# Attention times V as four column tiles with the attention weights moving, its denominators carried through DRAM, on one Trainium2 core

## The chip, the cores and the metric

The kernel runs on one core of one Trainium2 chip. The metric is the device time of one execution in microseconds (us), as the median of several runs. In these profiles PE is the tensor engine (PEld its weight loads), DVE the vector engine, ACT the scalar engine, POOL the general engine, and SP the engine that issues most DMAs. "L488" is line 488 of the kernel.

## The reference, cut to what matters

```python
x = A_x                                              # [1, 2048, 512], bf16
g = sigmoid((x * gate_w).sum(-1, keepdims=True))     # one gate per token
return g * attention(x) + (1 - g) * ffn(x)

# attention: 32 heads of 16, four segments of 512 tokens, for each segment
logits = einsum('bhqd,bhkd->bhqk', qs, ks) * scale + causal_mask
a_dot  = softmax(logits) @ vs                        # inside the segment
a_mem  = (phi(qs) @ M) / (phi(qs) . z + 1e-6)        # recall of earlier segments
o      = sigmoid(beta) * a_mem + (1 - sigmoid(beta)) * a_dot
M, z   = M + phi(ks)^T @ vs, z + phi(ks).sum()
# then o @ wo; ffn: (relu(x @ W_gate) * (x @ W_up)) @ W_down with 1792 hidden features
```

## The kernel before

A small planner in the kernel holds a list of tasks with engine, assumed duration, assumed latency, priority and dependencies. It fixes the order in which each engine's instructions are emitted. At run time every engine works through its list in that order, so an instruction whose input is late holds back those that follow on its engine (a stall of 6.19 us of this kind is shown below). Attention runs about two "units" (8 heads of one segment; in the trace one starts every 14.8 us on average) ahead of the feed-forward work, which fills the tensor engine.

`exp(logits)` is kept transposed, as E[key, query]. Attention times V takes E as the *stationary* operand and 17 columns (V and a column of ones, which yields the softmax denominator, "den") as the moving one. The result has queries on partitions, so that dens are per-partition columns and the combine is plain vector work:

```python
def pv(p=p, sl=sl):                      # p: half of the four query blocks
    for q2 in range(2):
        qb = 2 * p + q2
        if seg:                          # recall of earlier segments, beside it
            nc.tensor.matmul(wb[sl.banks[1]][:, q2 * 136:(q2 + 1) * 136],
                             lhsT=pqT[u % RQ][:, qb * P:(qb + 1) * P], rhs=mbd[i][:, c], ...)
        for h8 in range(8):
            j, r = divmod(h8, 2)
            for kb in range(qb + 1):
                ...
                nc.tensor.matmul(bank(sl)[:, lo:lo + HW],               # HW = 17
                                 lhsT=E[(5 * u + f) % RE][:, j, o:o + P],
                                 rhs=Vp[i][:, kb, 8 * c + h8, 0:HW], ...)
# comb(): reciprocal of den columns, times gates, times both products, add  (DVE)
# then a DMA transpose of the [query, feature] block into oT, for the matmul with wo
```

The softmax here doesn't subtract the row's maximum and nothing guards it: scores larger than these inputs give would overflow.

## Time and profile before

| | before |
|---|---|
| time, median (range) | 290.53 us (290.47 to 290.75) |
| span of the profiled run | 289.2 us |
| PE busy | 277.7 us, 96% |
| attention times V, first start to next start, summed (L488) | 34.4 us |
| all 512-column matmuls, likewise (L306) | 207 us |
| QK, row-tiled, likewise (L440) | 29.8 us |

Here are lines of the page of the kernel before: busy time per engine, then the busy tenths of PE in 40 slices of the span, the granted clock in tenths, and the chain that ended last by engine.

```profile
PE 277.7 (96%) x2860; PEld 138.3 (48%) x2906; DVE 176.5 (61%) x442; ACT 194.5 (67%) x168; POOL 87.3 (30%) x139
...
PE   8899999999999999999999999999999999899994
...
PEclk9999999999999999999999999999999999999999
...
PE 88%; ACT 3%; DMA 3%; issue 2%; another core or an unknown queue 1%; DVE 1%; SPq 0%; POOL 0%; ACTq 0%
```

PE is busy throughout, at full clock, and it makes up 88% of the chain: time taken from PE should come off the kernel.

The timeline of PE before (start us, duration us, engine, line, operation, out<-in, count) shows what one attention-times-V matmul and one change of tiling mode cost.

```profile
120.38 0.23 PE L479 MATMUL wb_135<-mbd_187,pqT_154 128*128 128x136 bf16 x1
120.45 0.17 PE L488 MATMUL wb_134<-Vp_163,E_82 128*128 128x17 bf16 x1
120.48 0.17 PE L488 MATMUL wb_134<-Vp_163,E_76 128*128 128x17 bf16 x1
120.50 0.17 PE L488 MATMUL wb_134<-Vp_163,E_78 128*128 128x17 bf16 x1
...
121.92 1.02 PE L306 MATMUL wb_133<-wv_sb,xT 128*128 128x512 bf16 x3
122.88 0.40 PE L440 MATMUL sp<-QT_137,KTe_143 32*128 32x384 bf16 x8
123.21 0.39 PE L306 MATMUL wb_132<-xT,wg_sb 128*128 128x512 bf16 x1
```

(Of the group of four that starts at 121.92, one record is missing.) A 17-column matmul takes 0.17 us, but one starts every 25 ns; busy times overlap, so distances between starts are what count. The QK group moves 512 columns in all and takes 0.33 us until the next start, where 512 columns in the plain mode take 0.216.

### The profile page before, as it was taken

How to read it: one execution, taken by the hardware profiler on the slowest of the kernel's cores; microseconds unless marked ns; L12 is line 12 of the kernel's file. 1: busy time of each engine (PE TensorE's matmuls, PEld its weight loads, DVE VectorE, ACT ScalarE, POOL GpSimd, SP SyncE). 2: the span in 40 equal slices, each digit the busy share in tenths (PEclk: the TensorE clock that was granted, in tenths of full speed). 3: DMA queues.
4: the chain of work that ended last, by engine and by line, in shares of the span. 5: the costliest groups of instructions: out<-in, count | busy, mean ns of one | idle time of the engine just before them, and what ended most of it. 6: DMA issues, size and time to landing. Idle time of an engine off the chain costs nothing.

```text
span 289.2 us, 6881 instructions
## 1 busy us (share of the span) xinstructions
PE 277.7 (96%) x2860; PEld 138.3 (48%) x2906; DVE 176.5 (61%) x442; ACT 194.5 (67%) x168; POOL 87.3 (30%) x139
## 2 busy tenths in 40 slices
PE   8899999999999999999999999999999999899994
PEld 4344546454545453545453545346635445544442
DVE  2689895666946168569692658657948434554211
ACT  2389888789865678779866678787796667433100
POOL 5025242333433334333334252423334243200000
PEclk9999999999999999999999999999999999999999
DMA  7999941010200201000103010000100111010011
GB/s 238 315 258 351 205 96 33 3 25 13 40 18 22 57 18 21 20 18 2 36 15 63 20 37 3 18 2 2 20 18 3 36 39 31 7 20 0 0 36 36
DMA packets 33198, 15.91 MB, mean 55 GB/s; under 512 B 22672, under 2 KB 33168, under 8 KB 33168
## 3 DMA queue, kind: packets, MB, share of 16 engines
q1 hardware_dynamic: 31424, 14.42, 20.2%
q10 hardware_dynamic: 1744, 1.06, 1.2%
q8 instruction: 22, 0.36, 0.6%
q14 instruction: 8, 0.07, 0.1%
HBM read 8.14 MB, written 2.10 MB: 35 GB/s over the span
## 4 chain that ended last, share of the span: by engine, by line
PE 88%; ACT 3%; DMA 3%; issue 2%; another core or an unknown queue 1%; DVE 1%; SPq 0%; POOL 0%; ACTq 0%
PE wb_133 L306 24%; PE wb_132 L306 20%; PE wb_135 L306 13%; PE sp L440 9%; PE wb_134 L306 8%; PE wb_134 L488 7%; DMA wk_sb<-in_A_wk_dram 3%; PE wb_132 L488 2%; PE wb_135 L488 1%; PE wb_135 L479 1%; ACT E_78 L461 1%; ACT E_76 L461 1%; ACT E_79 L461 1%; ACT E_77 L461 1%
## 5 line engine op out<-in xcount | busy, mean ns | idle before, releaser
L306 PEld LDWEIGHTS <-wu_sb 128*128 128x128 bf16 x224 | 20.2, 98 | 26.3 <-issue 4.9
L306 PEld LDWEIGHTS <-wg_sb 128*128 128x128 bf16 x224 | 19.9, 97 | 24.8 <-issue 4.5
L461 ACT ACTIVATE E_78<-sp 128x2048 bf16<-128x2048 f32 x10 | 18.8, 1877 | 7.0 <-PE sp L440 6.2
L306 PE MATMUL wb_132<-xT,wg_sb 128*128 128x512 bf16 x85 | 22.7, 380 | 0.4 <-issue 0.3
L461 ACT ACTIVATE E_83<-sp 128x2048 bf16<-128x2048 f32 x10 | 18.8, 1876 | 6.3 <-PE sp L440 6.1
L461 ACT ACTIVATE E_79<-sp 128x2048 bf16<-128x2048 f32 x10 | 18.8, 1876 | 6.0 <-PE sp L440 6.0
L461 ACT ACTIVATE E_76<-sp 128x2048 bf16<-128x2048 f32 x10 | 18.8, 1877 | 5.5 <-PE sp L440 5.1
L461 ACT ACTIVATE E_82<-sp 128x2048 bf16<-128x2048 f32 x10 | 18.8, 1875 | 5.5 <-PE sp L440 4.5
L461 ACT ACTIVATE E_77<-sp 128x2048 bf16<-128x2048 f32 x10 | 18.8, 1877 | 5.4 <-PE sp L440 3.3
L461 ACT ACTIVATE E_80<-sp 128x2048 bf16<-128x2048 f32 x10 | 18.8, 1876 | 4.8 <-PE sp L440 4.0
L461 ACT ACTIVATE E_81<-sp 128x2048 bf16<-128x2048 f32 x10 | 18.8, 1875 | 4.2 <-PE sp L440 4.1
L306 PE MATMUL wb_135<-xT,wu_sb 128*128 128x512 bf16 x68 | 18.5, 380 | 0.3 <-issue 0.2
L306 PE MATMUL wb_133<-xT,wu_sb 128*128 128x512 bf16 x68 | 18.5, 380 | 0.2
L467 POOL TENSOR_SCALAR_AFFINE_SELECT E_76<-E_76 128x512 bf16<-128x512 bf16 x16 | 10.4, 664 | 26.8 <-ACT E_76 L461 26.8
L467 POOL TENSOR_SCALAR_AFFINE_SELECT E_81<-E_81 128x512 bf16<-128x512 bf16 x16 | 11.7, 750 | 18.4 <-ACT E_81 L461 18.4
L467 POOL TENSOR_SCALAR_AFFINE_SELECT E_80<-E_80 128x512 bf16<-128x512 bf16 x16 | 10.9, 699 | 18.4 <-ACT E_80 L461 18.4
L467 POOL TENSOR_SCALAR_AFFINE_SELECT E_79<-E_79 128x512 bf16<-128x512 bf16 x16 | 10.2, 654 | 20.0 <-ACT E_79 L461 20.0
L467 POOL TENSOR_SCALAR_AFFINE_SELECT E_83<-E_83 128x512 bf16<-128x512 bf16 x16 | 10.0, 642 | 20.5 <-ACT E_83 L461 20.5
L467 POOL TENSOR_SCALAR_AFFINE_SELECT E_77<-E_77 128x512 bf16<-128x512 bf16 x16 | 10.4, 665 | 18.6 <-ACT E_77 L461 18.6
L467 POOL TENSOR_SCALAR_AFFINE_SELECT E_78<-E_78 128x512 bf16<-128x512 bf16 x16 | 10.0, 640 | 19.6 <-ACT E_78 L461 19.6
L467 POOL TENSOR_SCALAR_AFFINE_SELECT E_82<-E_82 128x512 bf16<-128x512 bf16 x16 | 10.0, 642 | 18.9 <-ACT E_82 L461 18.9
L582 ACT ACTIVATE rg<-wb_132 128x512 bf16<-128x512 f32 x22 | 13.1, 594 | 3.5 <-PE wb_132 L306 3.4
(539 smaller groups left out, 823.8 us busy)
## 6 DMA issues: line engine op xcount, KB each, us to landing
out_dram<-osb SPq DMA_DIRECT2D x16, 128.0 KB, 1.7
wd_sb<-in_B_W_down_dram SPq DMA_DIRECT2D x2, 896.0 KB, 8.2
wg_sb<-in_B_W_gate_dram SPq DMA_DIRECT2D x2, 512.0 KB, 9.3
wu_sb<-in_B_W_up_dram SPq DMA_DIRECT2D x2, 512.0 KB, 9.7
wg_sb<-in_B_W_gate_dram SPq DMA_DIRECT2D x2, 384.0 KB, 5.4
wu_sb<-in_B_W_up_dram SPq DMA_DIRECT2D x2, 384.0 KB, 5.2
wk_sb<-in_A_wk_dram SPq DMA_DIRECT2D x1, 512.0 KB, 7.5
wv_sb<-in_A_wv_dram ACTq DMA_DIRECT2D x1, 512.0 KB, 8.2
```

Source lines behind the costliest of these rows:

```text
L306: nc.tensor.matmul(bank(sl), lhsT=lhsT, rhs=rhs, start=(start and q == 0), stop=(stop and q == n - 1))
L440: nc.tensor.matmul(sp[:, j, off:off + n], lhsT=kt[32 * j:32 * j + 32, kb * P:(kb + 1) * P], rhs=QT[i][32 * j:32 * j + 32, kb * P:kb * P + ...
L461: b = plan.add("ACT", 1880, key, lambda Ef=Ef: nc.scalar.activation(Ef[:], sp[:], ACT.Exp, scale=SCALE), [a] + eread.get(n - RE, []), ACL)
L467: nc.gpsimd.affine_select(out=m, in_=m, compare_op=ALU.is_ge, fill=0.0, base=0, pattern=[[0, 4], [1, P]], channel_multiplier=-1)
L479: nc.tensor.matmul(wb[sl.banks[1]][:, q2 * 136:(q2 + 1) * 136], lhsT=pqT[u % RQ][:, qb * P:(qb + 1) * P], rhs=mbd[i][:, c], start=(q2 == 0 ...
L488: nc.tensor.matmul(bank(sl)[:, lo:lo + HW], lhsT=E[(5 * u + f) % RE][:, j, o:o + P], rhs=Vp[i][:, kb, 8 * c + h8, 0:HW], start=(q2 == 0 an ...
L582: nc.scalar.activation(rg[0][:], bank(sl), ACT.Relu)
```

## The change

V becomes the stationary operand (32 columns per head: 16 of V, one of ones, zeros) and E moves, up to 512 queries at a time. Four heads sit side by side in four column tiles of the array. A unit's 80 matmuls become two groups (even and odd heads) of 16. The result has features on partitions, as the matmul with wo wants it, so the transpose of the softmax part goes away. But dens are then *rows*, one per head. So that the reciprocal needn't run on single partitions, dens go through DRAM: out as rows, back as a compact [128, 32] tile, reciprocal and gates on DVE, out again, and back broadcast over 16 partitions per head. The odd heads' products are merged by four more DMAs. The token gates are needed in the compact layout too and also go through DRAM, as four stores of 512 single 4-byte elements. The recall is computed and combined apart. Memory is found by smaller rings (RQ, RH, and the staging tiles), by one buffer instead of two for the transposed keys pK, and by three segment buffers for x instead of four, with later loads. The planner also counts 100 ns for a change of tiling mode now, and 225 ns instead of 430 for a QK group.

```diff
-RQ = 6                         # query/key/feature buffers
+RQ = 5
-RH = 18                        # hidden buffers of the FFN
+RH = 16
...
+        for c in range(NC):    # head gates per partition: 2-byte elements
+            nc.sync.dma_start(out=betac[:, c:c + 1], in_=A_beta[8 * c:8 * c + 8]
+                                [:, None, None].to_broadcast([8, 16, 1]))
...
+        def rcd():             # token gates: 4-byte elements to DRAM
+                nc.sync.dma_start(out=rdram[seg].rearrange("(t p) -> p t", p=P),
+                                  in_=rcol[:, cols])
+        d = plan.add("SP", 500, key, rcd, [c], 2500)
+        att["rc", seg] = plan.add("SP", 500, key, lambda: nc.sync.dma_start(
+            out=rc[seg % 2][:], in_=rdram[seg].rearrange("(s n) -> s n", n=32)[None]
+            .to_broadcast([8, 16, 32])), [d] + war, 2500)
...
+            def pv(r=r, sl=sl):
+                for kb in range(4):
+                    f, o = EAT[r][kb]
+                    w = L - kb * P
+                    for j in range(4):
+                        nc.tensor.matmul(
+                            wb[sl.banks[0]][32 * j:32 * j + 32, kb * P:kb * P + w],
+                            lhsT=Vp[i][:, kb, 8 * c + 2 * j + r, :],
+                            rhs=E[(5 * u + f) % RE][:, j, o:o + w],
+                            start=(kb == 0), stop=(kb == 3), tile_position=(0, 32 * j))
...
+        def sp_task(dur, emit, deps, lat=2200):        # every hop: 2.2 us assumed
+            return plan.add("SP", dur, key, emit, deps, lat)
+        d0 = ...  ddram[u][0:8:2] <- ne[DH:P:32]       # dens of even heads
+        d1 = ...  ddram[u][1:8:2] <- no[DH - 1:P:32]   # dens of odd heads
+        merge = ... 4 x  ne[32j+16:32j+32] <- no[32j+16:32j+32]
+        a = sp_task(450, ld, [d0, d1])                 # dc <- ddram, [128, 32]
+        def cf():
+            nc.vector.reciprocal(dc[0][:], dc[0][:])
+            ... cc = dc * cgate * rc
+        ... cdram <- cc;  cT <- cdram, broadcast over 16 partitions
+                nc.vector.tensor_tensor(o1[0][:], ne[:], cT[:], ALU.mult)
```

## The prediction

> **What bounds it now.** TensorE. The page gives PE 277.7 of 289.2 us (96%) at full granted clock; DVE 61%, ACT 67%. The chain that ended last is 88% PE. Busy times overlap, so I split PE time by the distance from each matmul's start to the next one's (timeline, summed by line): projections and FFN (L306) 207 us, attention times V (L488) 34.4 us for 1280 matmuls of 128x17 at a median pitch of 25 ns, QK (L440) 29.8, memory update (L548) 3.1, recall (L479) 2.9.
>
> **What the change does on PE.** Per unit of 8 heads, 80 matmuls become 32: two groups of 4 key blocks x 4 column tiles, moving 512+384+256+128 = 1280 columns. A 512-column matmul has a pitch of 216 ns, so with four tiles together a group streams in about 535 ns. Entry and exit of a tiling mode I take from QK, which is row-tiled: the matmul before a QK group takes 312 ns instead of 216 (+96), the group 330 ns for 512 columns (+117). The Trainium skill ("TensorEngine Tiling (Array Packing)", Key Properties) says that changing the tiling mode drains the array; this trace agrees, with those 213 ns. Estimate: 535 + 213 = 750 ns per group, 32 groups, 24 us against 34.4: **minus 10.5 us**. That four column tiles overlap no run here shows yet; the skill ("TensorE: Matmul & The Clock Gate", Part 3) has 2.38x for three. Recall stays 48 matmuls; the memory update becomes 96 half-width ones: +0 to 0.5 us.
>
> **Other engines.** DVE loses the combine (two of about 1.9 us per unit) and gets the recall combine, one bank copy (690 ns), coefficients, a multiply and an add: roughly +5 us. ACT gets 16 copies of 600 ns: about 204 us. PSUM pressure falls: one bank for one copy instead of two for the combine. SP gets some 150 more DMAs. An issue takes about 0.45 us and a store lands in 1.7 us, so the chain dens out, in, coefficients out, broadcast in takes about 9-11 us per unit, SP's in-order queue blocked for much of it, against a unit period of about 14.8 us.
>
> **On the critical path.** All of the PE saving: PE is the limit from 9 us to the end; exps stop near 250 us and FFN work fills the rest, so late attention outputs have about two units of slack. The risk is in-order waits: coefficient and final multiply on DVE wait for DMAs; where these land later than scheduled, DVE holds PSUM banks and PE stalls. I allow 1-2 us for that and for the smaller rings (RQ 5, RH 16).
>
> **Time.** 290.5 - 10.5 + 1.5 = about 281.5 us, 80% range 275 to 289. Faster by over 2%: 0.63; within 2%: 0.27; slower: 0.10.
>
> **What would show it.** Right: an attention-times-V group 0.65-0.8 us from its first start to the next start, their sum 21-26 us; L306's work near 207 us; PE still 95% busy; DVE waits for coefficient and broadcast DMAs under 10 us. Wrong on overlap: groups of 1.3-2.1 us. Wrong on the side chain: group time as said, but DVE idle before the coefficient or final multiply, released by DMA, and new PE gaps released by DVE or ACT; broadcasts landing in over 4 us.
>
> **What would make it wrong.** 32-column weight loads that do not hide behind column-tiled matmuls; DMA hops of 3 us or more that accumulate on SP; ACT's extra copies delaying exps so that PE lacks filler at a segment's end. Upside: L306's roughly 6 us of stalls shrink with the bank pressure.

## The result, and the profile after

| | before | after |
|---|---|---|
| time, median (range) | 290.64 us (290.47 to 291.17) | 311.53 us (310.31 to 313.7) |
| PE busy | 277.7 us, 96% | 272.8 us, 88% |
| attention times V, start to next start | 34.4 us | 21.8 us |
| stretches without any matmul before the last one, summed | 7.7 us | 32.6 us |
| mean granted clock | 1.000 | 0.966 |

The ratio is 1.0724, with a 95% interval of 1.0656 to 1.0791. A ratio here is the mean time of one kernel's fast runs over that of the other's of the same rounds, so it isn't quite the ratio of the medians quoted. The change makes the kernel 7% slower.

The matmuls did what was expected. This is the timeline of PE after, around one unit's two groups:

```profile
137.21 0.59 PE L330 MATMUL wb<-xT,wg_sb 128*128 128x512 bf16 x2
137.73 1.27 PE L521 MATMUL wb<-E,Vp 128*32 128x512 bf16 x32
138.94 0.40 PE L481 MATMUL sp<-QT,KTo 32*128 32x512 bf16 x4
```

From 137.73 to 138.94, 1.21 us, both groups run: 2 x 1280 columns per tile, where four tiles taking turns would need four times 1.08 us (2560 columns at 216 ns per 512). The four tiles overlap, and their weight loads are hidden.

The same lines of the page after as of before:

```profile
PE 272.8 (88%) x2146; PEld 117.0 (38%) x2186; DVE 183.5 (59%) x425; ACT 202.8 (66%) x185; POOL 93.8 (30%) x143
...
PE   8879981999795398998989899999999999999995
...
PEclk9998996899999589999999999999999999999999
...
PE 51%; DMA 24%; DVE 11%; SPq 5%; issue 4%; ACT 3%; ACTq 0%; DVEq 0%
```

The PE row now has holes (1, 5, 3), the clock row has dips right behind them, and PE's share of the chain fell from 88% to 51%; DMA's rose from 3% to 24%. DVE and ACT are *less* busy, as shares, than before, though each has 7 to 8 us more work. Most of the loss is waiting, not work.

Waits after (who waited <- for what: us in total, times, longest us):

```profile
DVE dc L559 <- DMA dc<-ddram: 28.9, 10, 8.7
...
PE wb L330 <- DVE hT L682: 7.8, 2, 7.5
...
PE wb L330 <- DVE om L613: 7.0, 2, 6.2
...
DVE o L576 <- DMA coefT<-cdram: 5.7, 4, 2.2
...
ACT egate L273 <- DMA betac<-in_A_beta_dram: 2.5, 1, 2.5
```

DVE waits 28.9 us for dens to come back. PE then waits for DVE work that has nothing to do with dens (hT, om): it is only queued behind them. One such stall, in the timeline after (the last bracket is the idle time and what ended it):

```profile
93.94 0.54 SPq L389 DMA_DIRECT2D rdram<-rcol  x1
...
97.10 0.58 SPq L555 DMA_DIRECT2D dc<-ddram  x1
...
97.42 0.42 DVE L613 TENSOR_TENSOR om<-wb,cf 128x256 bf16<-128x256 f32 x1
...
99.14 0.40 PE L481 MATMUL sp<-QT,KTe 32*128 32x512 bf16 x4 [0.22 <-ACT E L502]
...
104.03 0.35 DVE L559 RECIPROCAL dc<-dc 128x32 f32<-128x32 f32 x1 [6.19 <-DMA dc<-ddram]
...
105.28 0.42 DVE L613 TENSOR_TENSOR om<-wb,cf 128x256 bf16<-128x256 f32 x1
...
105.76 1.87 PE L330 MATMUL wb<-wv_sb,xT 128*128 128x512 bf16 x4 [6.22 <-DVE om L613]
```

The token gates' 4-byte store (rdram) is issued at 93.94. The load of dens, issued at 97.10, reaches DVE only at 104.03. Behind it waits the recall combine `om`, which would have freed a PSUM bank, so PE stands for 6.22 us. Pieces of the chain after (start, us, what) show that such hops are slow at certain times only:

```profile
10.36 8.08 DMA betac<-in_A_beta_dram
...
33.22 12.57 DMA rdram<-rcol
...
49.77 1.93 DMA dc<-ddram
...
97.10 6.91 DMA dc<-ddram
...
111.05 8.64 DMA ddram<-numo
```

The same small load of dens takes 1.93 us at 49.77 and 6.91 at 97.10. The slow ones stand right behind the 4-byte stores, which are issued at 33.2, 33.8, 93.9 and 110.5. By the trace's packet records, the packets of the first two stores ran from about 36.3 to 36.8 us, after the last of the weight loads, and no packet at all ran from 43.7 until the first store landed at 45.8: most of its 12.57 us is not the moving of data.

Two stretches of the windows view after (us; busy us of PE, PEld, DVE, ACT, POOL; then clock, DMA share, GB/s) show a second loss:

```profile
20.00:60.00 40.00, 31.33 (x260) 12.64 (x265) 23.54 (x51) 26.92 (x29) 10.73 (x16) 0.87 0.73 151
...
100.00:140.00 40.00, 32.52 (x305) 14.32 (x310) 19.00 (x44) 24.26 (x19) 11.29 (x18) 0.87 0.23 57
```

The granted clock is 0.87 in these two stretches and 0.99 or 1.00 in the others. The trace's clock records give three stretches at half clock before the last matmul, of 3.4, 6.8 and 10.2 us, each beginning during or shortly after an idle gap. PE worked for about 11 us of them, so about 5 us were lost to the clock (an estimate from those records). The Trainium skill ("TensorE: Matmul & The Clock Gate", Part 1) says that the array falls back to half clock after an idle window of about 3.4 us. The lengths here are multiples of 3.4 us, as a window of that length would give; but the first stretch follows a gap of only 2.13 us, so less than a full idle window was enough.

A rough sum: 12.6 us less for the new matmuls, 25 us more of idle PE, about 5 us of half clock, and 18 entries into column tiling at 94 ns (1.7 us; the two groups of a unit mostly run back to back, with one entry for both). That makes +19, against +20.9 measured.

### The profile page after: what moved, and what is told of

It is laid out like the page before. It is cut to its first block, busy times and chain, and to the rows that moved or that the text cites. A ratio compares the mean times of both kernels' runs of the same rounds, so it can differ in the third digit from the quotient of the medians.

```text
span 309.0 us, 5730 instructions
## 1 busy us (share of the span) xinstructions
PE 272.8 (88%) x2146; PEld 117.0 (38%) x2186; DVE 183.5 (59%) x425; ACT 202.8 (66%) x185; POOL 93.8 (30%) x143
## 3 DMA queue, kind: packets, MB, share of 16 engines
q1 hardware_dynamic: 42208, 21.07, 28.9%
## 4 chain that ended last, share of the span: by engine, by line
PE 51%; DMA 24%; DVE 11%; SPq 5%; issue 4%; ACT 3%; ACTq 0%; DVEq 0%
PE wb L330 42%; DMA dc<-ddram 5%; PE sp L481 4%; DMA rdram<-rcol 4%; DMA coefT<-cdram 4%; PE wb L521 4%; SPq L547 3%; DMA ddram<-numo 3%; DMA betac<-in_A_beta_dram 3%; DMA wv_sb<-in_A_wv_dram 3%; ACT E L502 2%; DMA cdram<-cc 1%; DMA ddram<-nume 1%; DVE cf L612 1%; DVE hT L682 1%
## 5 line engine op out<-in xcount | busy, mean ns | idle before, releaser
L502 ACT ACTIVATE E<-sp 128x2048 bf16<-128x2048 f32 x80 | 150.2, 1877 | 38.7 <-PE sp L481 34.5
L508 POOL TENSOR_SCALAR_AFFINE_SELECT E<-E 128x512 bf16<-128x512 bf16 x128 | 82.5, 660 | 171.5 <-ACT E L502 167.2
L330 PE MATMUL wb<-xT,wu_sb 128*128 128x512 bf16 x215 | 57.8, 384 | 8.1 <-DVE hT L682 7.5
L330 PE MATMUL wb<-xT,wg_sb 128*128 128x512 bf16 x212 | 58.5, 386 | 2.4 <-DVE numo L537 0.9
L682 DVE TENSOR_TENSOR hT<-wb,rg 128x512 bf16<-128x512 f32 x56 | 38.4, 687 | 26.4 <-PE wb L330 17.7
L330 PE MATMUL wb<-wd_sb,hT 128*128 128x512 bf16 x216 | 52.5, 380 | 1.2 <-DVE QT L409 0.5
L676 ACT ACTIVATE rg<-wb 128x512 bf16<-128x512 f32 x56 | 33.2, 597 | 18.3 <-PE wb L330 17.4
L330 PEld LDWEIGHTS <-wu_sb 128*128 128x128 bf16 x224 | 20.9, 98 | 34.1 <-issue 11.6
L330 PEld LDWEIGHTS <-hT 128*128 128x128 bf16 x224 | 20.3, 98 | 26.3 <-issue 4.9
L521 PE MATMUL wb<-E,Vp 128*32 128x256 bf16 (+3 forms) x512 | 22.1, 311 | 2.1 <-DVE osb L705 1.4
L559 DVE RECIPROCAL dc<-dc 128x32 f32<-128x32 f32 x16 | 5.6, 349 | 28.9 <-DMA dc<-ddram 28.9
L481 PE MATMUL sp<-QT,KTe 32*128 32x512 bf16 (+3 forms) x256 | 17.5, 305 | 4.5 <-ACT E L502 4.0
L521 PEld LDWEIGHTS <-Vp 128*32 128x32 bf16 x512 | 11.9, 99 | 14.8 <-issue 4.6
L330 PE MATMUL wb<-xT,wq_sb 128*128 128x512 bf16 x61 | 16.5, 379 | 0.3 <-issue 0.3
L330 PE MATMUL wb<-wo_sb,oT 128*128 128x512 bf16 x61 | 16.5, 380 | 0.1
```

The costliest lines, as they stand in the source:

```text
L330: nc.tensor.matmul(bank(sl), lhsT=lhsT, rhs=rhs, start=(start and q == 0), stop=(stop and q == n - 1))
L481: nc.tensor.matmul(sp[:, j, off:off + n], lhsT=kt[32 * j:32 * j + 32, kb * P:(kb + 1) * P], rhs=QT[i][32 * j:32 * j + 32, kb * P:kb * P + ...
L502: b = plan.add("ACT", 1880, key, lambda Ef=Ef: nc.scalar.activation(Ef[:], sp[:], ACT.Exp, scale=SCALE), [a] + eread.get(n - RE, []), ACL)
L508: nc.gpsimd.affine_select(out=m, in_=m, compare_op=ALU.is_ge, fill=0.0, base=0, pattern=[[0, 4], [1, P]], channel_multiplier=-1)
L521: nc.tensor.matmul(wb[sl.banks[0]][32 * j:32 * j + 32, kb * P:kb * P + w], lhsT=Vp[i][:, kb, 8 * c + 2 * j + r, :], rhs=E[(5 * u + f) % RE ...
L559: nc.vector.reciprocal(dc[0][:], dc[0][:])
```

## The experiments

Four theories went in. **S**: the element-wise DMAs (4-byte gate stores, 2-byte loads of beta) hold up the side chain. **H**: every hop takes longer than the 2.2 us that the planner assumes, so the fixed orders are wrong everywhere. **R**: the smaller rings. **L**: more work on DVE and ACT. The ratios below compare with the kernel before on the same chip, 290.8 to 291.1 us; the differences between experiments are those of medians, some of them taken on different chips.

### e1_no_scatter: no 4-byte stores

```diff
+    for i in range(2):
+        nc.vector.memset(rc[i][:], 1.0)
-                nc.sync.dma_start(out=rdram[seg]..., in_=rcol[:, cols])
+                pass
-        att["rc", seg] = plan.add("SP", 500, key, lambda: nc.sync.dma_start(out=rc[seg % 2][:], ...
+        att["rc", seg] = plan.add("SP", 500, key, lambda: None, [d] + war, 2500)
```

> Wrong result on purpose: the row of token gates is a constant 1, and the four stores of 512 single 4-byte elements that carried it out, with the loads that brought it back, are gone; the schedule, all other DMAs and all vector work stay. Theory S (the element-wise stores hold up the side chain wherever they are in flight; the profile after shows the three long waits for dens, 8.7, 6.2 and 4.2 us, each beside one): the 7.5 and 6.2 us gaps on the tensor engine go, the clock stays whole after 30 us, 288 to 295 us. Theory H (every hop through DRAM is longer than the 2.2 us that the schedule assumes): 303 us or more, waits for dens still above 15 us. Theory R (smaller rings) and L (more vector and scalar work): no change, about 311 us.

Measured: 294.22 us (result wrong), 17.3 us less. Waits for dens fell from 28.9 to 8.5 us, with the longest 2.6. What remains in front is one 3.65 us gap at 18 us, behind the beta loads. S holds; H, R and L do not explain these 17 us. One clause missed: the clock did not stay whole after 30 us, with 3.4 us at half clock from 93 us.

### e2_no_dma_wait: DVE reads constants instead of the DMAs' results

```diff
-            nc.vector.reciprocal(dc[0][:], dc[0][:])
+            nc.vector.reciprocal(dr[:], dk[:])                  # dk: constant
-            ... dc[0][:], cgate[:, c:c + 1], rc[i][:] ...
+            ... dr[:], cgate[:, c:c + 1], dk[:] ...
-            nc.vector.tensor_tensor(o1[0][:], ne[:], cT[:], ALU.mult)
+            nc.vector.tensor_tensor(o1[0][:], ne[:], dk[:, 0:1].to_broadcast([P, L]), ALU.mult)
```

> Wrong result on purpose: reciprocal and final multiply read a constant, so that nothing on the vector engine waits for dens or for broadcast coefficients; every DMA is still issued. S and H alike: the tensor engine's gaps fall from 33 us to 10 or less, no half clock after 30 us, 278 to 284 us, which is what the matmul saving of 12.6 us alone would give. R and L: still above 300 us.

Measured: 297.24 us (wrong). The direction was right and the size was not: I expected 278 to 284. With DVE relieved, the delayed traffic struck elsewhere. The waits of this run show PE itself waiting for the transposed keys of the memory update:

```profile
PE wb L637 <- DMA pK<-pkT: 5.8, 1, 5.8
```

So DVE's wait was one path by which slow DMAs reached PE, and not the only one.

### e3_before_small_rings: the rings alone, in the kernel before

```diff
-RQ = 6
+RQ = 5
-RH = 18
+RH = 16
 # and two buffers instead of three for osb, kt and e1
```

> The kernel before with only the smaller rings of the change (5 query/key/feature buffers for 6, 16 hidden buffers for 18, two each of the exp, key and output staging tiles). S and H: 290 to 292 us. R: 296 us or more.

Measured: 294.31 us, ratio 1.0112 (1.009 to 1.0134). The rings cost the kernel before about 3.2 us. That lies between the two expectations: R is real, but it is a small part. The single pK buffer and the later loads of x are not in this run, and no run tests them alone.

### e4_plan_lat: only the planner's assumed latencies lengthened

```diff
-        def sp_task(dur, emit, deps, lat=2200):
-            return plan.add("SP", dur, key, emit, deps, lat)
+        def sp_task(dur, emit, deps, lat=4500):
+            return plan.add("SP", dur + 130, key, emit, deps, lat)
-        d = plan.add("SP", 500, key, rcd, [c], 2500)
+        d = plan.add("SP", 700, key, rcd, [c], 10000)
 # broadcast 2600 -> 5500; return of the gates 2500 -> 4500; gate inputs not before 19500
```

> Right result: the changed kernel, with only the schedule's assumptions lengthened (side-chain hops 4.5 us instead of 2.2, the broadcast 5.5 instead of 2.6, the gate row's store 10 instead of 2.5, an issue 0.58 instead of 0.45, the gate inputs not before 19.5 us), so that the in-order engines come to each wait later. H and S: waits for dens on the vector engine fall from 28.9 us to under 8, 280 to 290 us. R and L: about 311 us.

Measured: 305.29 us, a miss. That is 6.2 us less than the change, far from 280 to 290. DVE's waits for dens did fall, to 1.3 us, but PE waited for other things: 3.77 us at 20.9 us for a load of x, 2.35 us for the transposed keys of the memory update, and four times 1.5 to 2.2 us between 91 and 107 us for ACT's exps. The clock was 0.966 in the profiled run and up to 0.983 in the others. Planning around the stores, with these values, doesn't cure them.

```profile
PE wb L331 <- DMA xT<-in_A_x_dram: 3.8, 1, 3.8
...
DVE dc L560 <- DMA dc<-ddram: 1.3, 2, 0.9
```

### e6_scatter_unread: the stores stay, nobody reads them

```diff
+    for i in range(2):
+        nc.vector.memset(rc[i][:], 1.0)
-        att["rc", seg] = plan.add("SP", 500, key, lambda: nc.sync.dma_start(out=rc[seg % 2][:], ...
+        att["rc", seg] = plan.add("SP", 500, key, lambda: None, [d] + war, 2500)
```

> Wrong result on purpose: the element-wise stores of the token gates are issued as in the changed kernel, but nothing reads them: the coefficients use a constant 1. It tells whether the stores' traffic or the wait for their data costs the 17 us that went when both went. Traffic: the waits for dens near the stores stay, 300 us or more. Wait for the data: about 294 us as without the stores.

Measured: 308.21 us (wrong). Against e1 the only difference is that the four stores are issued. The waits for dens of e1, then of e6:

```profile
DVE dc L558 <- DMA dc<-ddram: 8.5, 8, 2.6
```

```profile
DVE dc L559 <- DMA dc<-ddram: 27.7, 9, 8.6
```

So about 14.0 us (308.21 - 294.22) come from the *traffic* of four 2-KB stores. The 3.3 us that are left for reading their data back (311.53 - 308.21) are hardly clear of the scatter: the runs span 307.87 to 310.62 here and 310.31 to 313.7 in the change.

### e7_early_gates_only: only the 2-byte loads of beta mended

```diff
-            nc.sync.dma_start(out=betac[:, c:c + 1], in_=A_beta[8 * c:8 * c + 8]...   # 4 x 128 elements
+        nc.vector.tensor_tensor(eg[:], ev, gv, ALU.mult)           # from the broadcast copy
+        nc.vector.tensor_tensor(eg[:], eg[:], bd[:, :, :, 0], ALU.mult)
+        nc.vector.tensor_reduce(out=cgate[:], in_=eg[:], op=ALU.add, axis=mybir.AxisListType.X)
 # gate weights and beta are loaded where the kernel before loads them
```

> Right result: the changed kernel with only the head-gate part mended (no 2-byte broadcast loads of beta, gate weights loaded early on the scalar queue); the 4-byte stores stay. S: the 2 to 3.7 us gap at 18 us and its half clock go, the later gaps stay: 3 to 8 us under the changed kernel, 303 to 308 us. H, R: 309 us or more.

Measured: 307.71 us, 3.8 us less, as expected. The gap at 18 us went; the later ones stayed. The edit both drops the 2-byte loads of beta and moves the gate weights' load to the front and onto ACT's queue; the 3.8 us are those of both.

### e5_dense_gates: both mended, with a right result

```diff
+        def split():                      # float32 gates as two bf16 parts
+            nc.vector.tensor_copy(rhi[:, cols], rcol[:, cols])
+            nc.vector.tensor_tensor(rlo[:, cols], rcol[:, cols], rhi[:, cols], ALU.subtract)
+        def tr():                         # [128, 4] -> [4, 128] on PE
+            for k, v in enumerate((rhi, rlo)):
+                nc.tensor.matmul(wb[ts.banks[0]][0:4, 0:P], lhsT=v[:, cols], rhs=ident[:], ...)
-                nc.sync.dma_start(out=rdram[seg].rearrange("(t p) -> p t", p=P), in_=rcol[:, cols])
+            nc.sync.dma_start(out=rdram[seg].rearrange("(t p) -> t p", p=P), in_=rT[:])
 # and the head gates as in e7
```

> Right result: the changed kernel without its element-wise DMAs. The token gates are turned into a [4, 128] row on the tensor engine (two matmuls of 128 columns per segment) and stored in four rows of 512 bytes; the per-partition head gates are built from the broadcast copy with the block mask; gate weights and beta load where the kernel before loads them. Theory S: as the run without the stores (294 us), less its 3.65 us gap at 18 us and the half clock behind it, 284 to 290 us. Theory H: 294 us or more.

Measured: 295.85 us (293.54 to 297.68), correct. That is 15.7 us less than the change, with the clock at 0.987 to 1.0, but it missed 284 to 290, and it is no better than e1, which still has the beta loads: the gains of e1 and e7 don't simply add. Waits for dens were still 12.7 us in this run, now spread over eight waits of at most 3.4 us. That points to H as a second part.

```profile
DVE dc L570 <- DMA dc<-ddram: 12.7, 8, 3.4
```

### e8_dense_lat: e5 with hop times as measured

```diff
-        def sp_task(dur, emit, deps, lat=2200):
-            return plan.add("SP", dur, key, emit, deps, lat)
+        def sp_task(dur, emit, deps, lat=3000):
+            return plan.add("SP", dur + 130, key, emit, deps, lat)
 # broadcast 2600 -> 3600
```

> Right result: the kernel with dense gates, and the schedule's side-chain hops set to what the profile after shows when nothing is in the way (about 3 us, the broadcast 3.6, an issue 0.58 us). H as a second part of the cause: 2 us or more faster than the dense kernel. S alone: within 2 us of it.

Measured: 291.89 us, 4.0 us less, on par with the kernel before (ratio 1.0041). The wait for dens is gone:

```profile
DVE dc L570 <- DMA dc<-ddram: 0.2, 1, 0.2
```

H is the second part of the cause. With the stores in place, longer planned hops had still left 305.29 us (e4).

### e9_bf16_side, e10_bf16_rings, e11_rings_lead, e12_dense_lead: towards a better version

```diff
 # e9 = e8 +
-    nume/numo/coefT = sb([P, L], F32, ...);  ddram/cdram = dram.tile([8, L], F32, ...)
+    nume/numo/coefT = sb([P, L], BF16, ...); ddram/cdram = dram.tile([8, L], BF16, ...)
 # e10 = e9 +
-RQ = 5
+RQ = 6
-RH = 16
+RH = 18
 # e11 = e10 +,  e12 = e8 +
-    LEAD, FLAG, RL = 2.0, 0.0, 40000.0
+    LEAD, FLAG, RL = 2.5, 0.0, 40000.0
```

> Right result within bf16: the kernel with dense gates and measured hops, with the side chain (evacuated products, dens, coefficients) in bf16 instead of float32; rings as in the change. It halves those DMAs' bytes and the final multiply's time. H (the rest of the loss is side-chain time) or L (vector work): 287 to 290 us, 2 us or more under the same kernel in float32 (291.9). R (the rest is the rings): 291 to 293 us.

> Right result: as e9_bf16_side, and the 6 kB that bf16 frees are given back to the rings (6 query/key/feature buffers, 18 hidden buffers, as in the kernel before). The smaller rings cost the kernel before 3.2 us. R: 3 us or more under e9_bf16_side, 284 to 288 us. H: within 1 us of it.

> Right result: as e10_bf16_rings, with attention 2.5 instead of 2 units ahead of the feed-forward work in the schedule, so that the side chain has half a unit (7 us) more. Meant as a version that beats both: 281 to 287 us. If slack for the side chain is no longer what is short, within 1 us of e10_bf16_rings.

> Right result: the float32 kernel with dense gates and measured hops (e8, 291.9 us), with attention 2.5 instead of 2 units ahead. H: 2 us or more under e8, 286 to 290 us. R: within 1 us of e8.

Measured, all correct: e9 289.41 us, e10 287.58, e11 287.05 (ratio 0.9864, 0.9849 to 0.9878), e12 288.16. A narrower side chain won 2.5 us, the old RQ and RH 1.8 (between the two expectations, 3 or more and at most 1), and half a unit more lead 3.7 without the other two (the runs of e12 scatter from 287.0 to 290.1) but only 0.5 on top of them, within the scatter. That suggests, but doesn't show, that all three buy the same slack. e11 just missed 281 to 287, and stayed within 1 us of e10, as expected if slack is no longer short. e9 singles out no theory, as bf16 changes bytes and vector time at once. The same page lines of e11:

```profile
PE 269.2 (94%) x2155; PEld 115.5 (41%) x2194; DVE 182.7 (64%) x437; ACT 201.3 (71%) x184; POOL 94.1 (33%) x143
...
PE   8898899999898899999999999999999999999995
...
PEclk9999999999999999999999999999999999999999
```

The holes and clock dips are gone, and e11 beats both kernels, by 1.4% over the kernel before.

### e13_scatter_on_act: the stores issued from another queue

```diff
-                nc.sync.dma_start(out=rdram[seg].rearrange("(t p) -> p t", p=P),
+                nc.scalar.dma_start(out=rdram[seg].rearrange("(t p) -> p t", p=P),
```

> Right result: the changed kernel (311.5 us), with only the four 4-byte stores issued from the scalar engine's queue instead of the sync engine's. Held up by the place in the queue: 295 to 302 us. Held up in the shared engines: 306 us or more.

Measured: 307.67 us, correct. A different queue won 3.9 of the 17 us; waits for dens were still 21.9 us:

```profile
DVE dc L559 <- DMA dc<-ddram: 21.9, 9, 8.9
```

So most of the hold-up is not one of places in SP's queue: it comes through what the queues share. The Trainium skill ("DMA: Bandwidth & Descriptors", Queues, rings and completion order) says that a DMA's semaphore increment lands only after every earlier write from the same DMA engine, across its queues. That fits a part of the delay. In the stall above, by the trace's packet records, half of the 128 packets of the load of dens had run by 98.59 us, the other half ran only from 100.98 to 101.29, and DVE went on only at 104.03; in the undisturbed load at 49.77 the last packet ended at 51.37 and DVE went on at 51.72. That the increment waited for receipts of the 4-byte writes is my reading of the 2.7 us after the last packet; no run shows it directly, and it doesn't explain the 2.4 us between the halves. In this stall it was not the engines' occupancy: they were busy for 28% of the time from 94 to 99 us, and the store's packets have a median of 7 ns each. At the first stores, from 34 to 46 us, the share was 72%, with packets of up to 4.5 us; there occupancy isn't excluded.

### e14_lead_scatter: the stores put back into e11

```diff
-            nc.sync.dma_start(out=rdram[seg].rearrange("(t p) -> t p", p=P), in_=rT[:])
+                nc.sync.dma_start(out=rdram[seg].rearrange("(t p) -> p t", p=P), in_=rcol[:, cols])
```

> Right result: the best kernel so far (e11, 287.05 us), with the 4-byte stores back in place of the four 512-byte rows; everything else, the order too, stays. S: slower by 6 us or more, 293 to 303 us. If the schedule was the true cause: within 2 us of e11.

Measured: 298.45 us, 11.4 us more than e11, with a 10.2 us stretch of half clock at 47 us. The same four stores cost 11 us in this schedule and 14 to 17 us (e6, e1) in that of the change.

### e15_double_pv: the new matmuls twice, in e11

```diff
-                for kb in range(4):
+                for kb in (0, 1, 2, 3) * 2:
```

> Right result: e11 with each column-tiled group issued twice over (the second pass starts the sum anew), 512 more matmuls of 1280 columns per four tiles and group, about 535 ns times 32 = 17 us of tensor time. If the tensor engine is the limit again: 302 to 307 us. If not, less than 10 us longer.

Measured: 302.79 us, correct, 15.7 us more than e11, or 0.49 us per group (the lower end of the expectation). The timeline of PE in this run has one unit's doubled groups:

```profile
137.19 2.36 PE L532 MATMUL wb<-E,Vp 128*32 128x512 bf16 x64 [0.27 <-DVE hT L694]
139.71 0.38 PE L329 MATMUL wb<-xT,wq_sb 128*128 128x512 bf16 x1 [0.16 <-issue]
```

In the mended kernel nearly all of the added tensor time (16.5 us, start to start) reaches the end, so the tensor engine is the limit again. That a saving there would count as fully is likely, but not what this run measures.

## Why the prediction was wrong, point by point

- **"PE is the limit", "minus 10.5 us".** Right. Predicted 750 ns per group with its entry; measured 21.8 us for 32 groups start to start, plus 18 entries of 94 ns (1.7 us in all) charged to the matmuls before. Four column tiles do overlap; the saving was about 11 us. That the sum came so close is in part luck: I had counted an entry for each of the 32 groups, and about 2.3 us of stalls and half clock inside the groups made up for the difference.
- **"I allow 1-2 us for that and for the smaller rings."** This is the step that failed. The term for late DMAs and rings measured some 31 us (311.5 against 290.5 - 10.5): 25 of idle PE, about 5 of half clock, and rest. I had named the path (DVE waits, holds PSUM banks, PE stalls) and mis-sized it.
- **"An issue takes about 0.45 us and a store lands in 1.7 us."** I took the landing time of a dense 128-KB store for every hop. Most undisturbed hops on the chain did take 1.4 to 4.2 us. But I never priced the two element-wise transfers in the diff by themselves: the first 4-byte store took 12.57 us, and the hops behind such stores 6.9 and 8.6. They cost 17.3 us (e1), of which about 14.0 by traffic alone (e6); the beta loads, with their place in the queue, cost 3.8 (e7).
- **The side chain against a 14.8 us unit.** Even with dense gates the planner's 2.2 us per hop was too short: 4.0 us (e8), and another 3.7 with half a unit more lead on top of that (e12).
- **"the smaller rings".** 3.2 us in the kernel before (e3), 1.8 in the mended one for RQ and RH alone (e10); within my 1 to 2 us for both risks there was no room for it.
- **The clock.** I left out that idle PE also loses its clock.
- **"DVE waits for coefficient and broadcast DMAs under 10 us", "PE still 95% busy".** 34.6 us and 88%: the profile signs that I had listed for "wrong on the side chain".

What stays open: by what mechanism the stores delay other DMAs (e13 leaves what the queues share). No run varied the size of the elements, their number or their destination one at a time, so which of these matters is open too. Then where 5.5 us lie between e11 (287.05) and the 281.5 predicted. In e11 PE is busy for 8.5 us less than in the kernel before, but idles 12.4 us before its last matmul instead of 7.7, mostly in short gaps before 100 us, many of them behind ACT and DVE; no run separates their shares.

## What to carry to other kernels

When a change turns an on-chip step into a chain of DMAs, price each transfer by its element size and by what else is in flight, not by the landing time of a large dense one: four stores of 512 single elements cost 11 to 17 us here, and a [128, 4] to [4, 128] turn, about 0.3 us of PE and 0.7 us of DVE a piece in e11, replaced them. On in-order engines a late DMA costs what is queued *behind* its reader, so look at what PE waits for next to what that engine waited for. Side-chain time, lead and ring space looked like exchangeable forms of slack here. Give the chain slack after its erratic part is gone, as one planned number cannot be right about a hop that takes 2 us at one time and 7 at another.

## What the Trainium skill lacked or had wrong

- "DMA: Bandwidth & Descriptors" says that transfers under 512 B do read-modify-write, and its rules advise against a non-contiguous last dimension, but it gives no cost of element-wise stores to *other* DMAs. Here a store of 512 x 4 bytes landed after 12.57 us, loads behind it took 6.9 us instead of 1.9, and issuing it from another queue won 3.9 of 17 us. Stores in 128-byte rows, also under 512 B, landed fast: the coefficients' store took 1.40 us in the chain.
- "TensorE: Matmul & The Clock Gate", Part 1, puts the fall to half clock after about 3.4 us of idling; it also reports a kernel whose clock oscillated with short idles, without their lengths. Here a gap of 2.13 us at 18.4 us was followed by 3.4 us at half clock, and in e1 gaps of 1.26 and 0.79 us close together were too, while in e11 a gap of 1.87 us at 27.7 us was not.
- The same page, Part 3 (What overlaps and what doesn't), says in its list that weight loads overlap running matmuls only when their row groups differ, though its text just above also names a background weight buffer. The column tiles here share all rows, and 32 loads with 32 matmuls of 2560 columns per tile took 1.21 us against 1.08 us of pure streaming, so they did overlap.
- The same part gives 2.38x for three column tiles; it has no figure for four with 128 rows, which ran at nine tenths of the full rate here (1.08 of 1.21 us).
